# A fused attention, gated MLP and soft mixture of experts: the last two experts in column halves, and all output in half rows

## The chip, the cores and the metric

The kernel runs on one core of a Trainium2 chip, as one launch. Its engines are named as in the profile: PE (TensorE, matmul) and PEld (its weight loads), DVE (VectorE), ACT (ScalarE), POOL (GpSimd) and SP (SyncE, which issues the transfers here). The metric is the time of the launch in microseconds (us), lower is better. Several executions of the kernel are timed, and one more is profiled. All arithmetic is in fp32.

## What is computed

The reference has three stages, the output of each being the input of the next:

```python
# 1 attention: q, k, v of (4, 12, 448, 64), q and k normalised by their RMS
x = softmax(q_n @ k_n.T / 8) @ v               # laid out as (1792, 768)
# 2 gated MLP, d_ff = 1536
x = (silu(x @ w_gate) * (x @ w_val)) @ w_out   # (1792, 768)
# 3 soft mixture of experts: 8 experts, 4 slots each, F = 1024
logits = x @ phi                               # (1792, 32)
d = softmax(logits, over the tokens)
slot_input = (d.T @ x).reshape(8, 4, 768)
for e in range(8):
    h = maximum(slot_input[e] @ w1[e], 0)      # w1[e]: 768 x 1024
    slot_out[e] = h @ w2[e]                    # w2[e]: 1024 x 768
c = softmax(logits, over the slots)
out = c @ slot_out.reshape(32, 768)            # (1792, 768)
```

Only 32 rows go through the experts, but each expert has 6.3 MB of weights of its own, 50.3 MB for the eight.

## The kernel before

The first 660 us or so are attention and the MLP, which the change does not touch. What it touches is the tail, written between `eunits` (L975) and the end of the kernel.

**Units.** The expert weights are cut into 32 units of 1.5 MB, listed in `eunits` as (expert e, kind i, half n). Kind 0 is half of w1[e], by rows. Kind 1 is half of w2[e], by rows: 512 rows of all 768 columns. Kind 2 is a column half of w2[e]: all 1024 rows of 384 columns. A unit's place in the list is the order both of its load and of its computation. Experts 0 to 6 have kinds 0, 0, 1, 1; the last, expert 7, has kinds 0, 0, 2, 2.

**Loads.** `load_unit(u)` (L1000) issues unit u on the SP queue into one of 16 buffers (`unit_tile`, L984). The units take the buffers in turn; three of the 16 are made of two or four smaller tiles, and a unit that falls on one of those is loaded in as many pieces. A unit of kind 2 is loaded in four pieces of 384 KB, one for two of the eight row groups `kh`, with runs of 384 numbers (1,536 bytes) (L1028 to L1030). The first sixteen units are loaded ahead of the loop; unit u + 16 is issued after the computation of unit u, so the last loads are issued, in program order, after unit 15. The output buffers `ot[b]` and the combine weights `ct` take buffers of earlier units.

**The loop over units (L1647).** Kind 0: the 32 slot rows times w1[e], 24 matmul records for each half, into `hacc[e]`; after the second half ACT applies the relu (L1666), PE transposes (L1669), and DVE copies the expert's four slots into `h1m`, whose other columns are zero (L1673). Kind 1: `h1m` times w2[e] (L1684), accumulated over the experts in one PSUM tile `so`; after the last of them DVE copies `so` to `sall` (L1692). Kind 2: `slot_open(n)` puts the column half n of `sall` into a new PSUM tile `sl[n]` (an identity product, L1595); `slot_last(n, kh)` adds expert 7's products (L1602), for eight `kh` of four products each; `slot_out(n)` copies the sums to `sos[n]` in SBUF (DVE, L1612).

**Output.** `output(n, b)` (L1616) makes column half n of batch b: eight products of `ct` with `sos[n]` into four PSUM tiles (L1629), four copies to `ot[b]`, two on DVE and two on ACT (L1636), and transfers. Batch b's 448 rows lie on 112 partitions with four rows each. For batches 0 and 1 each column half goes out by itself, in two transfers of 336 KB with runs of 1,536 bytes (L1641). Batches 2 and 3 go out once, after their second half, as whole rows in one transfer of 1,344 KB (L1643). In total there are eight of the small and two of the large. `outs` sets the order: for n = 0 batches 0, 1, 2, 3, for n = 1 batches 2, 3, 0, 1. Three outputs of n = 0 are made between the products of the last unit:

```python
slot_open(n)
for kh_ in range(KH):
    slot_last(n, kh_)
    if n == 1 and kh_ in (1, 3, 5):
        output(*outs[0].pop(0))
```

the other five after the loop.

**Order.** The section is under a manual schedule: each engine's queue runs in program order, and the waits on semaphores follow from which tiles are read and written. Transfers are all issued by SP, on one queue, with eight semaphores taken in turn. `fill(k)` (L128) issues k groups of four bf16 products on a zero tile, which nobody reads; here it stands behind the units from number 22 on that are not of kind 2, with three groups, and one behind unit `NE - 3`.

Of the kernel before, what the change touches and what calls it, by code (L numbers as in the profile page):

```python
# [21 lines left out]
def attn_moe_softmoe_kernel(  # L22
# [15 lines left out]
    nc = tc.nc  # L38
    B, H, S, HD = q.shape
# [3 lines left out]
    E, _, F = w1.shape  # L43
# [7 lines left out]
    KH = F // P  # L51
# [920 lines left out]
    KD2, KH2 = KD // 2, KH // 2  # L972


    eunits = [(e, i, n) for e in range(E) for i in (0, 2 if e == E - 1 else 1) for n in range(2)]  # L975
    NE = len(eunits)

    NR, NL = (9, 2), 5
# [462 lines left out]
    TF = [22, 3, 3]  # L1441
# [108 lines left out]
    with tc.manual_schedule():  # L1550
        tp_ = tc.alloc_tile_pool(name="tail", bufs=1, side="left", reuse_waits="tile")
        pools.append(tp_)
        for u in range(NRT - NG, NRT - NG + NL):
            load_unit(u)
        rs = tp_.tile([P, 1], F32, name="rs")
        nc.vector.tensor_scalar(out=rs, in0=ssum, scalar1=EPS_SUM, scalar2=None, op0=ALU.add)
        nc.vector.reciprocal(out=rs, in_=rs)
        si = tp_.tile([P, DM], F32, tag="si", name="si")
        for n in range(2):
            o = si[:, DH * n : DH * n + DH].rearrange("q (c p) -> q p c", c=KD2)  # L1560
            src = sip[n][:, :DH].rearrange("q (p c) -> q p c", c=KD2)
            if n:
                nc.vector.tensor_scalar(out=o, in0=src, scalar1=rs[:, 0:1], scalar2=None, op0=ALU.mult)
            else:
                nc.scalar.activation(out=o, in_=src, func=AF.Copy, scale=rs[:, 0:1])
        for u in range(NRT - NG + NL, NRT + NL):
            load_unit(u)
        sit_ps = pt_tile("sit")
        for c in range(KD):
            nc.tensor.matmul(  # L1570
                sit_ps[:, NS * c : NS * c + NS],
                si[:, P * c : P * c + P],
                stack[:, 0, :],
                start=True,
                stop=True,
            )
        sit = tp_.tile([P, KD, NS], F32, name="sit")
        nc.vector.tensor_copy(out=sit, in_=sit_ps[:, : KD * NS].rearrange("p (c s) -> p c s", c=KD))

        warm_tag[0] = "s2"  # L1580
        DQ = DM // 4
        sos = [tp_.tile([P, DQ], F32, name=f"sos{n}") for n in range(2)]
        sall = tp_.tile([P, DQ], F32, name="sall")
        so = ps.tile([P, DQ], F32, tag="g", name="so")
        FQ = F // 4
        hacc, h1s = {}, {}
        ot = {}
        sl = []

        def slot_open(n):  # L1590

            sl.append(ps.tile([P, DQ], F32, tag="vg"[n], name="sl"))
            for j in range(4):
                m = 2 * n + j % 2
                nc.tensor.matmul(  # L1595
                    sl[n][NS * j : NS * j + NS, :], ident[:, NS * m : NS * m + NS], sall, start=True, stop=False
                )

        def slot_last(n, kh):

            for j in range(4):
                nc.tensor.matmul(  # L1602
                    sl[n][NS * j : NS * j + NS, :],
                    h1s[E - 1][:, kh, :],
                    w(kh, DQ * (j % 2), DQ),
                    start=False,
                    stop=(kh == KH - 1),
                )

        def slot_out(n):  # L1610

            nc.vector.tensor_copy(out=sos[n], in_=sl[n])  # L1612

        ops_n = [0]

        def output(n, b):  # L1616

            if b not in ot:
                ot[b] = unit_tile(NE + 1 + b).rearrange("p (c d) -> p c d", d=DM)[:CP]
            ops = []  # L1620
            for _ in range(4):
                k = ops_n[0] % 6
                ops_n[0] += 1
                ops.append(s_tile(k) if k < 3 else pt_tile("op"))
            for c in range(2):
                for j in range(4):
                    r = slice(NS * j, NS * j + NS)
                    o = S * b + CP * (c + j // 2 * 2)
                    nc.tensor.matmul(  # L1629
                        ops[j][:CP, DQ * c : DQ * c + DQ], ct_()[r, o : o + CP], sos[n][r], start=True, stop=True  # L1630
                    )
            ob = out[S * b : S * b + S].rearrange("(p c) d -> p c d", c=NC)
            cs = slice(DH * n, DH * n + DH)
            for j in range(4):
                h = slice(j // 2 * 2, j // 2 * 2 + 2)
                (nc.scalar.copy if j % 2 else nc.vector.tensor_copy)(  # L1636
                    out=ot[b][:, h, DH * n + DQ * (j % 2) : DH * n + DQ * (j % 2) + DQ],
                    in_=ops[j][:CP, : 2 * DQ].rearrange("p (c d) -> p c d", d=DQ),
                )
                if j % 2 and b < 2:  # L1640
                    nc.sync.dma_start(out=ob[:, h, cs], in_=ot[b][:, h, cs])  # L1641
            if b >= 2 and n:
                nc.sync.dma_start(out=ob, in_=ot[b])  # L1643

        outs = [[(n, (b + 2 * n) % B) for b in range(B)] for n in range(2)]

        for u, (e, i, n) in enumerate(eunits):  # L1647
            w = wtile.pop(u)
            if i == 0:
                if n == 0:  # L1650
                    hacc[e] = s_tile(e % 3)[:, :FQ]
                for c in range(KD2 * n, KD2 * n + KD2):
                    for j in range(4):
                        nc.tensor.matmul(  # L1654
                            hacc[e][NS * j : NS * j + NS, :],
                            sit[:, c, :],
                            w(c % KD2, FQ * j, FQ),
                            start=(c == 0),
                            stop=(c == KD - 1),
                        )  # L1660
                if n == 1:

                    h1m = tp_.tile([P, KH, NS], F32, tag="h1m", name="h1m", bufs=2)
                    nc.gpsimd.memset(h1m, 0.0)
                    hr = tp_.tile([P, FQ], F32, tag="hr", name="hr", bufs=2)
                    nc.scalar.activation(out=hr, in_=hacc.pop(e), func=AF.Relu)  # L1666
                    ht_ = pt_tile("htp")
                    for t in range(2):
                        nc.tensor.transpose(  # L1669
                            ht_[:, P * t : P * t + P], hr.rearrange("q (p t) -> q t p", t=2)[:, t], ident  # L1670
                        )
                    for t in range(2):
                        nc.vector.tensor_copy(  # L1673
                            out=h1m.rearrange("p (j t) s -> p t j s", t=2)[:, t, :, SPE * e : SPE * e + SPE],
                            in_=ht_[:, P * t : P * t + P].rearrange("p (j s) -> p j s", j=4)[
                                :, :, SPE * e : SPE * e + SPE
                            ],
                        )
                    h1s[e] = h1m
            else:  # L1680
                if i == 1:
                    for kh_ in range(KH2 * n, KH2 * n + KH2):
                        for j in range(4):
                            nc.tensor.matmul(  # L1684
                                so[NS * j : NS * j + NS, :],
                                h1s[e][:, kh_, :],
                                w(kh_ % KH2, DQ * j, DQ),
                                start=(e == 0 and kh_ == 0),
                                stop=(e == E - 2 and kh_ == KH - 1),
                            )  # L1690
                    if e == E - 2 and n == 1:
                        nc.vector.tensor_copy(out=sall, in_=so)  # L1692
                else:
                    slot_open(n)
                    for kh_ in range(KH):
                        slot_last(n, kh_)
                        if n == 1 and kh_ in (1, 3, 5):
                            output(*outs[0].pop(0))
            load_unit(u + NRT + NL)
            if u == 1:  # L1700
                combine1(tp_)
            if CB + 2 <= u < CB + 2 + B:
                combine3(u - CB - 2)
            if CB <= u < CB + B:
                combine2(u - CB)
            if i == 2:
                slot_out(n)
            elif TF[0] <= u:
                fill(TF[1 + i] // (2 if u == NE - 3 else 1))
        for a in outs[0] + outs[1]:  # L1710
            output(*a)
    tp_.release()
# [32 lines left out]
```

## Time and profile before

| what | value |
|---|---|
| time, median of 3 runs | 778.86 us (777.36 to 779.46) |
| the profiled execution's own time | 779.32 us |
| its span | 777.5 us |
| PE, DVE, ACT, POOL busy | 731.6, 464.8, 391.3, 437.2 us |
| mean granted clock of TensorE | 0.977 |
| read from and written to HBM | 136.84 MB, 19.66 MB |

The span is what the trace covers; the own time is that of the same execution as the launch sees it, 1.8 us more. Times in rows count from the span's start. A matmul row merges neighbours: "x16" are sixteen records, and an fp32 product leaves two of them. "SPq" rows are SP's issue instructions, which end when the transfer is handed over and not when the data have landed. "Idle before" in square brackets is the time that the engine stood idle ahead of the row, with what ended it. The DMA share is the mean busy share of the core's 16 DMA engines; it can come out slightly over 1.

### The profile page before, as it was taken

The numbers are of one execution on the slowest core, as the hardware profiler recorded it, in microseconds if no ns is written. First come the engines' busy times: TensorE is split into PE (matmuls) and PEld (weight loads), VectorE is DVE, ScalarE is ACT, GpSimd is POOL, SyncE is SP. The second block draws the span as 40 slices with busy tenths as digits, with TensorE's granted clock in tenths as the row PEclk, the third lists the DMA queues.
The fourth block names the chain that finished last, engine by engine and source line by source line (L and its number), as shares of the span: only waits on it lengthen the run. The fifth ranks groups of instructions, "written<-read, shape, count | busy, mean of one in ns | idle before, by whom it ended". The sixth has DMA issues, their size and how long they took to land.

```text
span 777.5 us, 20479 instructions
## 1 busy us (share of the span) xinstructions
PE 731.6 (94%) x8488; PEld 567.2 (73%) x8488; DVE 464.8 (60%) x918; ACT 391.3 (50%) x834; POOL 437.2 (56%) x379
## 2 busy tenths in 40 slices
PE   7799999999999999999999999999999999888782
PEld 5565657787777777888888788888878887555451
DVE  5989877788877876676677766666342223210012
ACT  5889878887797644454454445443222221201012
POOL 5987765767676866778685686746234442001000
PEclk8899999999999999999999999999999999999986
DMA  7677675755585642545334443235158788999977
GB/s 229 171 240 197 204 220 188 224 180 187 178 269 174 195 120 77 155 141 153 85 119 120 142 137 78 82 108 161 51 194 298 273 327 314 362 416 417 417 276 241
DMA packets 72221, 157.84 MB, mean 203 GB/s; under 512 B 9184, under 2 KB 45280, under 8 KB 70368
## 3 DMA queue, kind: packets, MB, share of 16 engines
q1 hardware_dynamic: 72128, 156.52, 60.5%
q8 instruction: 67, 1.10, 0.6%
q14 instruction: 26, 0.21, 0.1%
HBM read 136.84 MB, written 19.66 MB: 201 GB/s over the span
## 4 chain that ended last, share of the span: by engine, by line
PE 79%; DMA 7%; DVE 5%; issue 3%; POOL 3%; ACT 2%; DVEq 0%; SPq 0%; ACTq 0%; POOLq 0%
PE pg L711 43%; PE s L508 6%; PE xp L645 6%; DMA w<-in_moe_w_dram 5%; PE tp L587 3%; PE tq L439 2%; PE s L610 2%; PE xp L610 2%; PE s L1654 2%; PE lp L763 2%; PE s L512 2%; PE sp L840 1%; DMA qk<-in_k_dram 1%; PE wpp L267 1%; PE so L1684 1%
## 5 line engine op out<-in xcount | busy, mean ns | idle before, releaser
L711 PE MATMUL pg<-xh,wh 128*128 128x448 f32 x576 | 219.5, 381 | 0.0
L711 PE MATMUL pg<-xl,wh 128*128 128x448 f32 x576 | 209.9, 364 | 0.0
L535 ACT ACTIVATE pr<-s,sm 128x448 f32<-128x448 f32 x168 | 106.2, 635 | 110.8 <-DVE sm L523 108.4
L711 PE MATMUL pg<-xh,wl 128*128 128x448 f32 x432 | 157.9, 366 | 0.3 <-POOL wl L254 0.3
L711 PEld LDWEIGHTS pg<-xh,wh 128*128 128x128 f32 x576 | 108.2, 188 | 23.0 <-issue 12.2
L254 POOL TENSOR_TENSOR wl<-raw,wh 128x768 fp32r<-128x768 f32 x60 | 111.0, 1860 | 16.2 <-ACT wh L246 16.0
L711 PEld LDWEIGHTS pg<-xl,wh 128*128 128x128 f32 x576 | 108.5, 188 | 8.2 <-issue 0.6
L246 ACT CAST wh<-raw 128x768 fp32r<-128x768 f32 x96 | 78.9, 835 | 65.6 <-PE pg L711 34.3
L552 POOL TENSOR_SCALAR pr<-pr,su 128x448 f32<-128x448 f32 x84 | 54.5, 659 | 80.7 <-DVE su L548 34.7
L523 DVE TENSOR_REDUCE sm<-s 128x1 f32<-128x448 f32 x168 | 97.7, 613 | 2.7 <-PE s L508 0.9
L218 POOL TENSOR_TENSOR hpos<-hpos,hneg 128x768 f32<-128x768 f32 x36 | 66.1, 1836 | 37.1 <-ACT hneg L209 32.8
L711 PEld LDWEIGHTS pg<-xh,wl 128*128 128x128 f32 x432 | 81.2, 188 | 7.6 <-POOL wl L254 0.7
L732 DVE SCALAR_TENSOR_TENSOR ht<-ht,pg 128x448 f32<-128x448 f32 x48 | 29.7, 619 | 77.6 <-ACT ht L725 77.4
L254 POOL TENSOR_TENSOR raw<-raw,wh 128x768 fp32r<-128x768 f32 x24 | 44.1, 1840 | 51.2 <-ACT wh L246 51.2
L391 POOL TENSOR_TENSOR ri<-ss,mhalf 128x16 f32<-128x16 f32 (+2 forms) x24 | 67.3, 2802 | 2.0
L508 PE MATMUL s<-ka,qa 64*128 64x448 f32 x432 | 64.0, 400 | 1.7 <-DVE ka L65 0.9
L587 PE MATMUL tp<-ident,pr 128*112 128x128 f32 x336 | 51.6, 286 | 6.6 <-ACT pr L535 4.8
L631 DVE STREAM_TRANSPOSE pT<-pr 128x448 f32<-128x448 f32 x84 | 52.7, 628 | 5.3 <-POOL pr L552 5.1
L587 PEld LDWEIGHTS tp<-ident,pr 128*112 128x112 f32 x336 | 37.7, 137 | 23.4 <-ACT pr L535 8.6
L711 PE MATMUL pg<-xh,raw 128*128 128x448 f32 x144 | 52.7, 366 | 0.8 <-POOL raw L254 0.8
L508 PEld LDWEIGHTS s<-ka,qa 64*128 64x128 f32 x432 | 35.3, 186 | 23.1 <-issue 12.4
L413 POOL TENSOR_TENSOR qn<-qk,ri 128x512 f32<-128x512 f32 (+1 forms) x46 | 50.2, 1090 | 0.7
(190 smaller groups left out, 1158.4 us busy)
## 6 DMA issues: line engine op xcount, KB each, us to landing
w<-in_moe_w_dram SPq DMA_DIRECT2D x24, 1536.0 KB, 12.6
raw<-w SPq DMA_DIRECT2D x72, 384.0 KB, 4.9
w<-raw SPq DMA_DIRECT2D x36, 384.0 KB, 4.0
vt<-in_v_dram SPq DMA_DIRECT2D x60, 224.0 KB, 4.2
r<-in_moe_w_out_dram SPq DMA_DIRECT2D x12, 768.0 KB, 5.0
r<-in_moe_w_gate_dram SPq DMA_DIRECT2D x12, 768.0 KB, 5.3
r<-in_moe_w_val_dram SPq DMA_DIRECT2D x12, 768.0 KB, 5.9
w<-in_moe_w_dram SPq DMA_DIRECT2D x8, 768.0 KB, 15.1
```

The source lines that it names most:

```text
L218: eng.tensor_tensor(out=hp, in0=hp, in1=hn, op=ALU.subtract)
L246: (EV[ENG["wh1"]] if u - NO < NU else nc.scalar.copy)(out=wh, in_=wst[u]["raw"])
L254: eng.tensor_tensor(out=wl, in0=wst[u]["raw"], in1=wst[u]["wh"].bitcast(F32), op=ALU.subtract)
L391: nc.gpsimd.tensor_tensor(out=ri, in0=ss, in1=mhalf[:p, : len(ns)], op=ALU.pow)
L413: eng.tensor_tensor(out=st[i]["qn"][:, n].rearrange("p c h d -> p h c d"), in0=st[i]["qk"][: rows(i), n], in1=st[i]["ri"][:, n] .rearrange ...
L508: nc.tensor.matmul(sc[j], qa[r, wt, c * P : (c + 1) * P], ka[r, mv, :], start=(n == 0), stop=(n == 2))
L523: nc.vector.tensor_reduce(out=d["sm"][:, j : j + 1], in_=d["sc"][j], axis=AX.X, op=ALU.max, negate=True)
L535: nc.scalar.activation(out=p, in_=d["sc"][j], func=AF.Exp, bias=d["sm"][:, j : j + 1], accum_out=st[i]["su"][:, c, j : j + 1])
L552: nc.gpsimd.tensor_scalar(out=p, in0=p, scalar1=su[:, j : j + 1], scalar2=1.0, op0=ALU.mult, op1=ALU.mult)
L587: nc.tensor.transpose(tp[:CP, ck * P : (ck + 1) * P], pr[:, ck * CP : (ck + 1) * CP], ident)
L631: nc.vector.transpose(out=pT[:, 6 - c if j else c, :], in_=st[i][c]["pr"].pop(j))
L711: nc.tensor.matmul(d[r], wt[:, P * c : P * c + P], mv, start=(c == 0 and n == 0), stop=(c == KD - 1 and n == 2),)
```

## The change

The last two experts are treated alike. The list of units becomes: experts 0 to 5 as before; then both halves of the first weights of expert 6, then those of expert 7; then the first column halves of the second weights of experts 6 and 7, then the second column halves of the two. `so` and `sall` now end with expert 5. `slot_open(n)` runs at expert 6's column half, `slot_last` takes the expert as an argument, and `slot_out(n)` comes after expert 7's column half. During the second column halves of experts 6 and 7 an output of n = 0 is made ahead of `kh` 0 and `kh` 4, four in all, each ahead of two pairs of weight pieces. All batches now go out as half rows, sixteen transfers of 336 KB, in the order of the batches for both halves. The filling products end with unit 27 (`NE - 5`), which has one group.

```diff
@@ -972,7 +972,9 @@
     KD2, KH2 = KD // 2, KH // 2
 
 
-    eunits = [(e, i, n) for e in range(E) for i in (0, 2 if e == E - 1 else 1) for n in range(2)]
+    eunits = [(e, i, n) for e in range(E - 2) for i in range(2) for n in range(2)]
+    eunits += [(e, 0, n) for e in (E - 2, E - 1) for n in range(2)]
+    eunits += [(e, 2, n) for n in range(2) for e in (E - 2, E - 1)]
     NE = len(eunits)
 
     NR, NL = (9, 2), 5
@@ -1596,15 +1598,15 @@
                     sl[n][NS * j : NS * j + NS, :], ident[:, NS * m : NS * m + NS], sall, start=True, stop=False
                 )
 
-        def slot_last(n, kh):
+        def slot_last(e, n, kh, w):
 
             for j in range(4):
                 nc.tensor.matmul(
                     sl[n][NS * j : NS * j + NS, :],
-                    h1s[E - 1][:, kh, :],
+                    h1s[e][:, kh, :],
                     w(kh, DQ * (j % 2), DQ),
                     start=False,
-                    stop=(kh == KH - 1),
+                    stop=(e == E - 1 and kh == KH - 1),
                 )
 
         def slot_out(n):
@@ -1637,12 +1639,10 @@
                     out=ot[b][:, h, DH * n + DQ * (j % 2) : DH * n + DQ * (j % 2) + DQ],
                     in_=ops[j][:CP, : 2 * DQ].rearrange("p (c d) -> p c d", d=DQ),
                 )
-                if j % 2 and b < 2:
+                if j % 2:
                     nc.sync.dma_start(out=ob[:, h, cs], in_=ot[b][:, h, cs])
-            if b >= 2 and n:
-                nc.sync.dma_start(out=ob, in_=ot[b])
-
-        outs = [[(n, (b + 2 * n) % B) for b in range(B)] for n in range(2)]
+
+        outs = [[(n, b) for b in range(B)] for n in range(2)]
 
         for u, (e, i, n) in enumerate(eunits):
             w = wtile.pop(u)
@@ -1686,16 +1686,17 @@
                                 h1s[e][:, kh_, :],
                                 w(kh_ % KH2, DQ * j, DQ),
                                 start=(e == 0 and kh_ == 0),
-                                stop=(e == E - 2 and kh_ == KH - 1),
+                                stop=(e == E - 3 and kh_ == KH - 1),
                             )
-                    if e == E - 2 and n == 1:
+                    if e == E - 3 and n == 1:
                         nc.vector.tensor_copy(out=sall, in_=so)
                 else:
-                    slot_open(n)
+                    if e == E - 2:
+                        slot_open(n)
                     for kh_ in range(KH):
-                        slot_last(n, kh_)
-                        if n == 1 and kh_ in (1, 3, 5):
+                        if n == 1 and kh_ % 4 == 0:
                             output(*outs[0].pop(0))
+                        slot_last(e, n, kh_, w)
             load_unit(u + NRT + NL)
             if u == 1:
                 combine1(tp_)
@@ -1703,10 +1704,10 @@
                 combine3(u - CB - 2)
             if CB <= u < CB + B:
                 combine2(u - CB)
-            if i == 2:
+            if i == 2 and e == E - 1:
                 slot_out(n)
-            elif TF[0] <= u:
-                fill(TF[1 + i] // (2 if u == NE - 3 else 1))
+            elif i < 2 and TF[0] <= u:
+                fill(TF[1 + i] // (2 if u == NE - 5 else 1))
         for a in outs[0] + outs[1]:
             output(*a)
     tp_.release()
```

## Rows read from the trace of the kernel before

**Rows 1.** The page's head, and its DMA rate in 40 equal slices of the span (GB/s).

```profile
span 777.5 us, 20479 instructions
...
GB/s 229 171 240 197 204 220 188 224 180 187 178 269 174 195 120 77 155 141 153 85 119 120 142 137 78 82 108 161 51 194 298 273 327 314 362 416 417 417 276 241
```

**Rows 2.** TensorE and DMA by stretches: busy us of each engine, clock, DMA share, GB/s.

```profile
720.00:740.00 20.00, 14.26 (x223) 9.07 (x220) 0.61 (x3) 1.45 (x3) 0.31 (x1) 1.00 1.03 417
738.00:742.00 4.00, 1.62 (x29) 0.76 (x26) 0.00 (x0) 0.00 (x0) 0.00 (x0) 0.99 1.00 419
743.00:749.00 6.00, 4.65 (x42) 2.33 (x42) 0.26 (x2) 0.38 (x1) 0.00 (x0) 0.52 1.07 373
751.00:755.00 4.00, 4.00 (x92) 2.79 (x88) 1.38 (x3) 0.86 (x2) 0.00 (x0) 1.00 0.05 17
756.00:759.00 3.00, 2.99 (x60) 1.92 (x52) 2.04 (x5) 1.44 (x4) 0.00 (x0) 1.00 1.01 314
760.00:761.00 1.00, 0.79 (x18) 0.48 (x14) 0.98 (x2) 0.85 (x2) 0.00 (x0) 1.00 0.07 21
764.00:769.00 5.00, 0.00 (x0) 0.00 (x0) 0.75 (x2) 0.63 (x2) 0.00 (x0) 0.68 0.99 352
772.00:774.00 2.00, 0.00 (x0) 0.00 (x0) 0.00 (x0) 0.00 (x0) 0.00 (x0) 0.50 0.95 323
```

**Rows 3.** The chain of waits from 640 us: start us, us, what.

```profile
701.84 25.49 DMA w<-in_moe_w_dram
...
727.40 17.00 DMA w<-in_moe_w_dram
```

**Rows 4.** Timeline, SP queue from 725 us: start us, us, line, transfer, count.

```profile
729.27 15.68 SPq L1030 DMA_DIRECT2D w<-in_moe_w_dram  x8
754.41 2.71 SPq L1641 DMA_DIRECT2D out_dram<-w  x4
...
763.09 8.39 SPq L1641 DMA_DIRECT2D out_dram<-w  x4
```

**Rows 5.** Source lines 1030 (its issues, their landing) and 1641: ns min/median/max, starts.

```profile
L1030 SPq DMA_DIRECT2D w<-in_moe_w_dram x8: 540/546/5354, 729.3 to 744.4; - x8
...
DMA to landing us min/median/max: 8.2/13.6/16.2
...
L1641 SPq DMA_DIRECT2D out_dram<-w x8: 317/998/2632, 754.4 to 768.9; - x8
```

**Rows 6.** DMA issues of outputs at 754.41, 763.09, 768.9: KB, us to landing.

```profile
out_dram<-w SPq DMA_DIRECT2D x1, 336.0 KB, 2.8
...
out_dram<-w SPq DMA_DIRECT2D x1, 336.0 KB, 10.6
...
out_dram<-w SPq DMA_DIRECT2D x1, 336.0 KB, 7.7
```

**Rows 7.** Timeline, TensorE, four stretches of matmuls: start us, us, shape, count.

```profile
712.82 1.48 PE L1654 MATMUL s<-w,sit 128*32 128x256 f32 x24
...
744.44 2.79 PE L1654 MATMUL s<-w,sit 128*32 128x256 f32 x24 [0.79 <-DMA w<-in_moe_w_dram]
...
752.09 0.83 PE L1602 MATMUL sl<-w,h1m 128*32 128x192 f32 x16
...
753.70 0.86 PE L1602 MATMUL sl<-w,h1m 128*32 128x192 f32 x16
```

**Rows 8.** Timeline, VectorE, copies of the slot sums and of outputs.

```profile
752.01 0.36 DVE L1612 COPY sos<-sl 128x192 f32<-128x192 f32 x1 [3.15 <-PE sl L1602]
753.79 1.02 DVE L1636 COPY w<-s 112x384 f32<-112x384 f32 x2 [1.42 <-PE op L1629]
...
762.47 1.02 DVE L1636 COPY w<-s 112x384 f32<-112x384 f32 x2 [0.24 <-PE s L1629]
763.73 0.56 DVE L1636 COPY w<-op 112x384 f32<-112x384 f32 x1 [0.23 <-PE op L1629]
```

**Rows 9.** Waits of the SP queue from 725 us: us, times, longest.

```profile
SPq L1030 <- DMA w<-in_moe_w_dram: 7.5, 7, 3.1
```

## The prediction

> **What bounds the kernel now.** I read the page's head first, then the DMA rate by stretches, the chain of waits, the SP queue, and last TensorE and VectorE in the final 40 us. The slices of the page [rows 1] show a rate of 416 and 417 GB/s shortly before the end, falling to 276 and 241 in the last two. The stretches [rows 2] say what that is: from 720 to 740 us the queue moves 417 GB/s at a full share, from 743 to 749 us 373 GB/s, also at a full share, and then from 751 to 755 us only 17 GB/s. The chain [rows 3] names DMA alone for 701.84 to 744.40 us: the weights of the eight experts stream in, and everything else waits for them. So the weight stream sets the time until about 751 us. After it comes a hole, because the outputs cannot start: the reader is to see in the SP rows [rows 4] that the loads are issued by 744.95 us and the first output only at 754.41 us. In between TensorE does the last expert: its first-layer product at 744.44 us in 2.79 us, the relu and transposes, 64 slot matmuls, and the first combine products [rows 7]. From 754.41 us on the queue is fed piecewise: 21 GB/s from 760 to 761 us, since the two whole-row transfers wait for both column halves. The last four half-row transfers are issued from 763.09 us, the last one at 768.9 us, and it lands 7.7 us later, at 776.6 us [rows 4 to 6]; the span ends 0.9 us behind it.
>
> I therefore treat the tail as one queue: bytes at a known rate, plus holes.
>
> **Part 1: experts 6 and 7 by column halves.** No weight byte is added. The first weights of both experts come first (four units), then four units of column halves, two of which used to be whole-row units. Column-half pieces (384 KB, 1,536 B runs) go at 373 GB/s, the pieces before them at 417 [rows 2]. Two units are 3.146 MB: 8.43 us instead of 7.54, so 0.9 us more. The last weight landed at 744.4 + 8.2 = 752.6 us (the last start and the shortest landing [rows 5]) and now lands at 753.5. SP issues six more loads; its issue instructions run far ahead of the data (the last is done at 744.95 us, 7.7 us before that piece lands), so they are hidden. If that cover failed, each would cost its some 0.5 us.
>
> The pieces land 1.02 us apart (the first of the eight at 729.27 + 16.2 = 745.5 us, the longest landing; the last at 752.6 [rows 4, 5]), so the last piece of the first column half of expert 7 lands 8 x 1.02 us before the end, at 745.3 us, and expert 7's first layer arrives before all sixteen, at about 737.2. Between that product's end (747.23 us) and the first slot matmul's readiness (752.01 - 3.15 = 748.86) lay 1.6 us [rows 7, 8]; this now has some 5 us of room before expert 7's first half is due, and leaves the end's path. That is the heart of the change: before, 1.6 us of hand-over, 128 slot matmuls and the combine stood behind the last first-layer weight.
>
> **Part 2: TensorE behind the weights.** The slot matmuls are 256 instead of 128, but expert 6 no longer has its 64 + 64 in the old form, so the number of products is the same. Two chunks of 16 matmuls take 0.83 and 0.86 us, and from one chunk's start to the next there were 1.61 us with a batch's combine between them [rows 7], so that the combine takes 0.77 us (1.61 less a chunk's mean). From 745.3: a chunk 0.86, the copy of the slot sums 0.36 [rows 8], the combine 0.77, and 0.62 from the copy's start (753.79) to the issue (754.41) [rows 4, 8]. The first output transfer is issued at 748.0 us. Each further batch follows after two chunks and a combine, 2.46 us: 750.5, 752.9, 755.4. The last chunk ends at 746.6 + 4 x 2.46 = 756.4 us; it is TensorE's pace, not the landing at 753.5, that sets this. Copy, combine and eviction put the first transfer of the second half at 758.2, and the others follow at 1.26 us (762.47 to 763.73, VectorE's pace [rows 8]).
>
> **Part 3: all output as half rows.** Ten output transfers become sixteen of 336 KB. What one costs in a full queue: the last four landed from 763.09 + 10.6 = 773.7 to 776.6 us, 0.97 us each [rows 4 to 6]; 314 and 323 GB/s [rows 2] mean 1.10 and 1.07. I take 1.05. Whole rows went at 352 GB/s, so their 2.75 MB lose 0.7 us; this is within the 1.05.
>
> Are the outputs ever late? An output on an empty queue landed 2.8 us after its issue [rows 6]. If the queue runs on without a hole, output k lands at 753.5 + 1.05 k. Batch 0 needs its issue by 754.55 - 2.8 = 751.7 and has it at 748.0, 3.7 us early. The next have 3.3, 3.0 and 2.6 us, and the first of the second half 1.9 us (due at 760.1, there at 758.2). After that batches come every 1.26 us and leave every 2.1. SP's own waits: its column-half loads waited for the landing of earlier loads seven times [rows 9], one landing for each issue, eight apart; in that pattern output 1 waits for the piece that lands at 746.4 and output 8 for the last weight at 753.5, both before the data of those outputs are ready. All loads stand ahead of all outputs in SP's order, so no load waits behind an output's data. On an output that waits, only later outputs are queued.
>
> **Sum.** Last landing 753.5 + 16 x 1.05 = 770.3 us, 0.9 us to the end: a span of 771.2 instead of 777.5, 6.3 us less. Against its own time, 779.32, that is 773.0 us. The median of the runs is 778.86, inside their spread of 2.1 us; I leave the small difference to hand-overs that are not perfect. With 0.97 and 1.10 per transfer the sum gives 771.7 and 773.8.
>
> What the change costs on the queue is 0.9 + 0.7 us; what it fills is the hole from 751 to 755 us, the slow start and the second hole at 760.
>
> A rule that speaks against it: the Trainium skill (Perfetto Trace Analysis, DMA Optimizations) says that transfers under 2 KB carry a large overhead each and that batching them to 4 or 8 KB can raise throughput dramatically. By the rule the outputs should suffer most. The trace agrees in sign, with 373 against 417 GB/s for loads and 314 to 323 against 352 for stores [rows 2], but not in size.
>
> **Rivals.**
> *A, the clock dips once more (774.5 us).* From 738 to 742 us TensorE was busy 1.62 of 4.00 us, waiting for a 1.5 MB unit, and from 743 to 749 the granted clock was 0.52, half speed [rows 2]; 24 matmuls took 2.79 us there against 1.48 [rows 7]. The same idle stretch does not arise in the changed order (four small pieces instead of a large unit at that place, with 0.83 us of matmuls per 1.02 us), but the warm-up matmuls after these units are gone as well. A dip as long as the one seen, some 7 us, makes TensorE 3.4 us late; 1.9 us are free, so 1.5 us are left: 774.5.
> *B, half rows are dearer in a long row of them (776.5 to 781 us).* It eats the whole gain only if one takes 1.05 + 6.3/16 = 1.44 us, 239 GB/s; the slowest full stretch shows 314. Against it: four in a row kept 1.10.
> *C, slower: the clock stays at half from the first slot matmul on (785 us).* Chunks then take 1.69 us, more than the 1.02 us of a piece, and TensorE takes the place of the queue: 8 chunks from 739 us end at 752.5, then four times 4.9 us, copy, combine and eviction: the second half's first issue at 775.0, three batches at 1.5 us and a landing of 2.8 put the last landing near 782.8 and the time at about 785.5. It decides once TensorE loses over 6.3 + 1.9 = 8.2 us, which is more than 16 us at half speed. Against it: after the dense first-half products the clock is 1.00 from 751 us on [rows 2], and the new order is dense from 739.
> The Trainium skill (TensorE: Matmul & The Clock Gate, HAM oscillation) describes such a loop: compute shorter than the wait for its next slice throttles the array again and again. This trace shows the single dip.
> *D, outputs cut into the last loads.* The four transfers issued before 753.5 could delay the last weight by 4.2 us, to 757.7; the second half's first issue would then be 757.7 + 0.86 + 0.36 + 0.77 + 0.62 = 760.3, against a due time of 760.1: 773.2, no other result.
>
> **Chances.** The forecast with D, 771 to 774: 0.74. A and other small lateness, 774 to 776.5: 0.13. B or anything else that ends within 0.3% (2.3 us, about what this measurement can tell from no change): 0.07. C and slower: 0.06. So faster 0.87, same 0.07, slower 0.06. The range for 8 in 10 is 771.0 to 776.5: below it lies 0.97 us per transfer together with the median's 0.46 us, above it the dip with 1.10 us per transfer and a lost hand-over.
>
> **What the changed profile would show.** Right: no stretch below 280 GB/s between 740 and 768 us; slot matmuls from about 739 us and a clock of 1.00 through 757; first output issued near 748, last load landed near 753.5, last output near 770. Wrong: a hole around 752 or 760 (TensorE late, A or C: then the clock row says 0.5), output pieces over 1.2 us apart (B), or the last weight later than 755 (D).

## The result, and the profile after

The changed kernel took 768.96 us (median of 6 runs, 768.01 to 771.62), the kernel before in six runs 777.01 us (773.76 to 779.46): the ratio is 0.9903, with a 95% interval of 0.9873 to 0.9932. Timed once more, over 12 runs, it was 769.81 us against 774.77, a ratio of 0.9934 (0.9910 to 0.9959). The change is faster, as forecast, by 0.7 to 1.0%. The forecast of 773.0 us and its range of 771.0 to 776.5 are above the measured time.

The page's head and the DMA rate in 40 slices, of the changed kernel:

```profile
span 766.8 us, 20577 instructions
...
GB/s 232 167 244 188 224 224 194 229 176 189 163 271 195 195 99 104 146 132 141 84 123 156 145 81 81 116 132 132 84 145 241 316 305 335 310 415 417 416 376 308
```

The last two slices are 376 and 308 GB/s where they were 276 and 241 [rows 1]. The stretches tell the same in detail (columns as in [rows 2]):

```profile
700.00:726.00 26.00, 22.18 (x384) 14.42 (x378) 0.87 (x5) 2.90 (x6) 3.21 (x7) 1.00 1.02 419
736.00:742.00 6.00, 5.21 (x112) 3.02 (x108) 0.00 (x0) 0.00 (x0) 0.00 (x0) 1.00 1.07 373
745.00:749.00 4.00, 4.00 (x88) 2.63 (x84) 1.18 (x3) 0.97 (x3) 0.00 (x0) 1.00 1.08 382
750.00:754.00 4.00, 3.52 (x76) 2.47 (x68) 1.41 (x4) 0.86 (x2) 0.00 (x0) 1.00 1.05 374
755.00:764.00 9.00, 2.58 (x43) 1.65 (x36) 3.07 (x6) 2.58 (x6) 0.00 (x0) 0.77 0.98 314
```

Neither hole of [rows 2] is left: the DMA share is 0.98 or more in each of these stretches. Column-half loads go at 373 GB/s, as before. TensorE's clock is 1.00 as long as it has work in these stretches; there is no dip like that of 743 to 749 us in [rows 2]. New is the difference between the two output stretches, 374 GB/s and then 314. The first still holds the end of the loads; from 752 to 755 us, with outputs alone, the rate is 368.

The SP queue (start, duration, line, count), and the sources of its transfers with their issue times and time to landing:

```profile
721.87 20.33 SPq L1032 DMA_DIRECT2D w<-in_moe_w_dram  x16
744.58 17.68 SPq L1643 DMA_DIRECT2D out_dram<-w  x16
```

```profile
L1643 SPq DMA_DIRECT2D out_dram<-w x16: 317/422/1190, 744.6 to 761.7; - x16
...
DMA to landing us min/median/max: 4.1/5.2/8.1
```

The first output is handed over at 744.58 us, right behind the loads; before it was 754.41, 9.5 us behind them [rows 4]. The last load was issued at 741.65 us and landed 9.8 us later, at 751.4; six outputs stood in the queue by then. On TensorE and VectorE the chain that the prediction followed can be read directly:

```profile
738.59 1.84 PE L1604 MATMUL sl<-w,h1m 128*32 128x192 f32 x32 [0.27 <-DMA w<-in_moe_w_dram]
740.62 0.86 PE L1604 MATMUL sl<-w,h1m 128*32 128x192 f32 x16 [0.20 <-DMA w<-in_moe_w_dram]
...
751.04 1.51 PE L1604 MATMUL sl<-w,h1m 128*32 128x192 f32 x32
```

```profile
742.60 0.36 DVE L1614 COPY sos<-sl 128x192 f32<-128x192 f32 x1 [7.29 <-PE sl L1604]
743.95 1.02 DVE L1638 COPY w<-s 112x384 f32<-112x384 f32 x2 [0.99 <-PE op L1631]
...
752.62 0.36 DVE L1614 COPY sos<-sl 128x192 f32<-128x192 f32 x1 [0.47 <-PE sl L1604]
```

Up to 741 us TensorE waits for each piece (0.2 us at a time, ended by DMA); from the first copy of the sums on it waits for no load any more and sets its own pace to the second copy at 752.62.

**Two parts of the difference.** The profiled execution is 10.7 us shorter, more than the medians differ. A place up to which the two programs are the same is the last piece of expert 6's first weights; let M be its landing. The matmuls that wait for it, in the kernel before, in the changed kernel, and in the changed kernel's second profile:

```profile
729.26 1.06 PE L1654 MATMUL s<-w,sit 128*32 128x256 f32 x12 [0.82 <-DMA w<-in_moe_w_dram]
```

```profile
725.60 1.06 PE L1654 MATMUL s<-w,sit 128*32 128x256 f32 x12 [0.81 <-DMA w<-in_moe_w_dram]
```

```profile
729.05 1.06 PE L1654 MATMUL s<-w,sit 128*32 128x256 f32 x12 [0.77 <-DMA w<-in_moe_w_dram]
```

M is 729.2, 725.55 and 729.0 us. So 3.65 us of the 10.7 lie in M, up to which the two programs are the same, and 7.05 behind it: from M to the end of the span, which I call the tail, 48.3 us became 41.25. In the second profiles the tails were 47.6 (before) and 41.2 us (after).

### The profile page after: what moved, and what is told of

Same layout as the page of the kernel before. It is cut to its first block, busy times and chain, and to the rows that moved or that the text cites. A ratio compares the mean times of both kernels' runs of the same rounds, so it can differ in the third digit from the quotient of the medians.

```text
span 766.8 us, 20577 instructions
## 1 busy us (share of the span) xinstructions
PE 728.0 (95%) x8528; PEld 565.6 (74%) x8528; DVE 465.1 (61%) x918; ACT 391.7 (51%) x834; POOL 437.7 (57%) x379
## 4 chain that ended last, share of the span: by engine, by line
PE 77%; DMA 10%; DVE 4%; issue 3%; POOL 3%; ACT 2%; DVEq 0%; SPq 0%; POOLq 0%; ACTq 0%
PE pg L711 44%; DMA w<-in_moe_w_dram 8%; PE s L508 6%; PE xp L645 6%; PE tp L587 4%; PE tq L439 2%; PE xp L610 2%; PE s L610 2%; PE lp L763 2%; PE s L512 2%; PE sp L840 1%; PE wpp L267 1%; DMA qk<-in_k_dram 1%; PE rb L570 1%; DMA w<-raw 1%
## 5 line engine op out<-in xcount | busy, mean ns | idle before, releaser
L254 POOL TENSOR_TENSOR wl<-raw,wh 128x768 fp32r<-128x768 f32 x60 | 111.1, 1861 | 14.6 <-ACT wh L246 14.4
L587 PEld LDWEIGHTS tp<-ident,pr 128*112 128x112 f32 x336 | 37.0, 135 | 24.2 <-ACT pr L535 9.4
```

Of the source, the lines that this page charges most:

```text
L254: eng.tensor_tensor(out=wl, in0=wst[u]["raw"], in1=wst[u]["wh"].bitcast(F32), op=ALU.subtract)
L587: nc.tensor.transpose(tp[:CP, ck * P : (ck + 1) * P], pr[:, ck * CP : (ck + 1) * CP], ident)
```

## The experiments

Each is compared by its tail, which came out within 0.1 us in the two profiles of the changed kernel and within 0.7 in those of the kernel before, and by its ratio to the kernel before on the same chip. The tail of the first four expectations was counted from the copy of `sit`. That copy turned out a poor mark: it came at 674.7 to 681.0 us in the first six profiles without the weight stream moving along with it. The numbers below are from M; the differences that were expected carry over. Counted from the copy, as they were written, the four tails are 95.3, 95.3, 93.0 and 98.4 us.

| run | tail from M, us | first output issued, us after M | ratio to before (95%) |
|---|---|---|---|
| before, two profiles | 48.3, 47.6 | 25.2, 24.7 | 1 |
| changed, two profiles | 41.25, 41.2 | 19.0, 19.2 | 0.9903 (0.9873 to 0.9932), 0.9934 (0.9910 to 0.9959) |
| order_only | 45.0 | 19.0 | 0.9977 (0.9959 to 0.9995) |
| halves_only | 46.0 | 25.4 | 0.9969 (0.9947 to 0.9992) |
| late_out | 48.5 | 27.7 | 1.0014 (0.9996 to 1.0031) |
| two_queues | 40.9 | 19.0 | 0.9927 (0.9901 to 0.9952) |
| late_two | 50.8 | 28.3 | 1.0043 (1.0026 to 1.0060) |
| pe_late | 42.7 | 19.0 | 0.9952 (0.9932 to 0.9973) |
| one_expert | 45.2 | 24.2 | 0.9997 (0.9977 to 1.0017) |
| no_fill | 40.9 | 19.0 | 0.9942 (0.9921 to 0.9964) |
| one_per_half | 41.2 | 19.5 | 0.9935 (0.9914 to 0.9956) |

Each edited kernel has one profile, so its tail is one execution. In seven of the sets, the second one of the changed kernel among them, the ratio shows 0.8 to 2.9 us less gain than the tails do; no run shows where that difference lies.

**The kernel before again.** No edit.

> The kernel before, unchanged, profiled once more. Marker: the copy of `sit` on VectorE, with which the experts begin; head = span start to marker (678.4 us before, 674.7 after the change), tail = marker to span end (99.1 and 92.1). Theory H: the head is the same code in both kernels and only differs between executions (the kernel before had half-clock stretches at 114 and 670 us, the changed one had not); then head anywhere from 673 to 679, tail 99.1 +- 0.8. Rival: the change itself shortened the head by 3.7 us; then head 678.4 +- 0.5 again.

By the mark of this expectation theory H missed: the copy came at 678.9 us, in the rival's range, and the tail from it was 95.3 instead of 99.1. M decides it: it came at 726.5 us, 2.7 earlier than in the first profile of the same kernel, and the tail from it was 47.6. In all thirteen profiles of this text, of kernels with the same code up to M, M lies between 724.4 and 731.3 us. The rival falls: what lies ahead of M varies from execution to execution by 6.9 us, about as much as the change gains.

**The new order alone.**

```diff
-                if j % 2:
+                if j % 2 and b < 2:
                     nc.sync.dma_start(out=ob[:, h, cs], in_=ot[b][:, h, cs])
+            if b >= 2 and n:
+                nc.sync.dma_start(out=ob, in_=ot[b])
-        outs = [[(n, b) for b in range(B)] for n in range(2)]
+        outs = [[(n, (b + 2 * n) % B) for b in range(B)] for n in range(2)]
```

> The new order of experts and the interleaved outputs, but the old output form (batches 0, 1 as half rows, 2, 3 as whole rows at the end, old order of batches). Queue theory: after the last weight only four half-row transfers are ready, the queue runs dry for some 2.3 us until the whole rows come: tail 92.1 + 3.6 = 95.7 us (95 to 96.5), first output issued as in the changed kernel. Rival, the order alone makes the gain and the form of the output is of no weight: tail 92 to 92.8.

The tail is 3.75 us over the changed kernel's. The hole stands where it was expected, between the four half rows and the whole rows:

```profile
755.00:758.00 3.00, 3.00 (x68) 1.82 (x58) 1.33 (x3) 1.05 (x3) 0.00 (x0) 1.00 0.79 289
758.00:760.00 2.00, 1.23 (x20) 0.92 (x20) 0.94 (x3) 0.55 (x2) 0.00 (x0) 1.00 0.13 44
760.00:762.00 2.00, 1.76 (x31) 1.45 (x32) 1.53 (x4) 1.20 (x4) 0.00 (x0) 1.00 0.54 172
764.00:769.00 5.00, 0.00 (x0) 0.00 (x0) 0.21 (x1) 0.09 (x1) 0.00 (x0) 0.64 1.00 355
```

**Half rows alone.** The inverse edit, on the kernel before. It changes the form of the output and the order of the batches together; no run separates the two.

> The old order of experts with all output as half rows in the order of the batches. Queue theory: the hole behind the weights stays (first output 1.8 us after the last weight landed), but the second hole goes, and sixteen transfers of 0.97 to 1.10 us follow each other: tail 99.1 - 2.5 to 4.4 = 94.7 to 96.6 us. Rival, only the expert order matters: tail 99 +- 0.5.

A gain of 1.6 to 2.3 us in the tail, less than the 2.5 to 4.4 expected: the hole behind the weights stays, and the sixteen transfers land 1.12 us apart, not 0.97 to 1.10.

```profile
751.00:753.00 2.00, 2.00 (x44) 1.31 (x44) 1.25 (x3) 1.05 (x3) 0.00 (x0) 1.00 0.18 47
756.00:760.00 4.00, 3.26 (x56) 2.24 (x50) 3.25 (x7) 2.72 (x7) 0.00 (x0) 1.00 1.02 320
```

Each part alone brings some 3 and 2 us, both together 6.4 to 7.1.

**Outputs behind the last product.**

```diff
                     for kh_ in range(KH):
-                        if n == 1 and kh_ % 4 == 0:
-                            output(*outs[0].pop(0))
                         slot_last(e, n, kh_, w)
```

> The changed kernel, but all eight outputs are made after the last slot product instead of four between weight pieces. Queue theory: the queue runs dry when the weights end, the first output is issued some 2 us after the last weight has landed instead of 7 us before: tail 92.1 + 5.3 = 97.4 us (96.4 to 98.4). Rival, the bytes alone set the end: tail 92 to 92.8.

The whole gain is gone: a tail of 48.5 us, as in the kernel before. So the new order of the experts by itself gains nothing; it pays through the outputs that it lets issue while weights still load. The loss of 7.3 us is 2 us more than expected. The hole is there, and then the transfers land 1.14 us apart for the whole of the output:

```profile
753.00:756.00 3.00, 2.55 (x52) 1.50 (x44) 1.12 (x3) 0.72 (x2) 0.00 (x0) 1.00 0.00 0
757.00:774.00 17.00, 6.13 (x92) 4.28 (x92) 6.64 (x14) 5.55 (x14) 0.00 (x0) 0.76 1.00 303
```

**The changed kernel again.** No edit.

> The changed kernel, unchanged, timed beside the kernel before on one chip. New marker M: the first of the last twelve matmuls of expert 6's first layer (729.26 us before, 725.60 after), since the copy of `sit` came at 678 to 681 us in four further profiles while the weight stream behind it did not move; tail M = M to the span's end (48.2 before, 41.2 after). Theory H: the change works only behind M; tail M 41.2 +- 0.6, M itself anywhere between 725 and 732, and the median lies 6.4 to 7.1 us under the kernel before. Rival: it also shortens what lies ahead of M; then 8 us or more.

The tail repeats to 0.1 us, and M was 3.5 us later than in the first profile. The medians differ by 5.0 us here and by 8.1 in the first set; with the ratios' intervals both hold a gain of 6.4 to 7.0 us. The rival, something gained ahead of M, is not supported.

**Two queues.**

```diff
-                    nc.sync.dma_start(out=ob[:, h, cs], in_=ot[b][:, h, cs])
+                    (nc.scalar if n and j == 3 else nc.sync).dma_start(out=ob[:, h, cs], in_=ot[b][:, h, cs])
```

> The changed kernel, with every second output transfer of the second half issued from ScalarE's queue instead of SP's. In the changed kernel the transfers that SP issues one after the other take 0.85 to 1.2 us each to hand over there, and land 0.96 us apart, while the first half's, issued ahead, landed 0.87 apart. Theory I (the hand-over of one queue paces them): the second half lands 0.87 to 0.90 us apart, tail M 40.4 +- 0.3. Rival D (the write rate of the DMA engines paces them): 0.96 apart, tail M 41.2 +- 0.3. Rival: ScalarE's copies wait behind its issues, 41.5 and more.

The second half landed from 758.18 to 765.12 us, 0.99 apart: no gain. The tail of 40.9 us is inside the rival's range. The hand-over got shorter and the landing did not, so theory I is not what paces the output here.

**Two queues for late output.** The same with `j == 3` for both halves, on the kernel with late outputs.

> All eight outputs after the last slot product (as in the run with late outputs, tail M 48.5, sixteen landings 1.14 us apart), with every second transfer from ScalarE's queue. Theory I: landings about 0.9 apart, tail M 44.9. Rival D: 1.14 apart, tail M 48.5 +- 0.5.

1.24 us apart and a tail of 50.8, outside both ranges: slower still. Theory I falls. Of the 2.3 us over late_out, 0.6 lie ahead of the first output, which was issued 28.3 us after M instead of 27.7; that the second queue causes the rest is seen in this one profile.

**TensorE late.**

```diff
             if i == 2 and e == E - 1:
+                if n:
+                    fill(12)
                 slot_out(n)
```

> The changed kernel with 48 warm-up matmuls (some 3.3 us of TensorE) put ahead of the last copy of the slot sums. Prediction's margin: the second half's first transfer is issued 754.6 us and could land 2.8 us later, at 757.4, but lands at 759.1; so 1.7 us are free and the tail M is 41.2 + 1.6 = 42.8. Rival I (the hand-over paces the second half, so nothing is free): 41.2 + 3.3 = 44.5. Rival, the end is set by bytes alone: 41.2.

The fill took 2.85 us, partly beside the copy that TensorE waits for anyway, and put the second half's first issue 2.0 us later (31.1 us after M instead of 29.0). That transfer landed 0.3 to 0.6 us later, as a margin of 1.7 us allows. But the queue was short of work for a while, 243 GB/s at a DMA share of 0.68 from 752 to 756 us, and the seven behind it came 1.13 us apart instead of 0.96 to 0.99, so the tail grew by 1.5 us. The total agrees with the first expectation, the way there does not.

```profile
749.00:752.00 3.00, 3.00 (x64) 2.30 (x61) 1.38 (x3) 0.86 (x2) 0.00 (x0) 1.00 1.06 387
752.00:756.00 4.00, 3.68 (x68) 3.27 (x67) 1.02 (x2) 0.86 (x2) 0.00 (x0) 1.00 0.68 243
756.00:764.00 8.00, 2.47 (x40) 1.54 (x34) 3.06 (x6) 2.58 (x6) 0.00 (x0) 0.93 0.95 290
```

**Only expert 7 by column halves.**

```diff
-    eunits += [(e, 2, n) for n in range(2) for e in (E - 2, E - 1)]
+    eunits += [(E - 2, 1, n) for n in range(2)] + [(E - 1, 2, n) for n in range(2)]
-                        if n == 1 and kh_ % 4 == 0:
+                        if n == 1 and kh_ % 2 == 0:
```

(`so` and `sall` end with expert 6 again, `slot_open` is at expert 7.)

> A version meant to beat both: expert 7's first weights ahead of expert 6's second weights, but only expert 7 by column halves (expert 6's second weights as whole rows, at 417 instead of 373 GB/s), the four outputs of the first half each ahead of one pair of row groups of the last unit, output all as half rows. Queue theory with the measured prices: the weights end 0.9 us earlier; TensorE has only one unit to make four outputs in, so the first output of each half lands up to 0.4 us behind its turn: tail M 40.7 (40.3 to 41.2). Rival, one unit is too short a cover and TensorE paces the end: tail M 42 and more.

The rival holds, and more: a tail of 45.2 us. The weights landed at 24.8 us after M, no earlier than the 24.6 to 25.9 of the changed kernel. The first output came 5 us later and the queue ran dry. In the trace the products of expert 6's second weights start at 737.29 us, after a wait of 1.78 us that the landing of a 1.5 MB unit ended, and the clock dips as in the kernel before; that these two make the delay is read from the trace and not tested. The ratio of 0.9997 shows no gain in the time at all:

```profile
730.00:740.00 10.00, 6.71 (x78) 3.60 (x74) 0.26 (x2) 0.38 (x1) 0.00 (x0) 0.75 1.02 405
740.00:745.00 5.00, 5.00 (x92) 3.83 (x92) 0.36 (x1) 0.00 (x0) 0.00 (x0) 0.81 1.07 374
745.00:750.00 5.00, 4.85 (x108) 3.27 (x104) 1.39 (x4) 0.86 (x2) 0.00 (x0) 1.00 0.48 164
```

**No fill.** The calls of `fill` behind units 24 to 27 left out.

> The changed kernel without the warm-up matmuls behind units 24 to 27. Rival A of the prediction (a dip of the clock makes TensorE late, 1.7 us are free): a granted clock of 0.5 for some us between 728 and 745 and a tail M of 41.2 to 43. If the dense slot products alone hold the clock: no dip, tail M 41.2 +- 0.2.

No dip, and a tail of 40.9 us, 0.3 less. TensorE was idle for more than half of 728 to 732 us and the clock stayed:

```profile
728.00:732.00 4.00, 1.59 (x16) 0.70 (x14) 0.26 (x2) 0.38 (x1) 0.00 (x0) 1.00 0.98 404
736.00:740.00 4.00, 3.08 (x58) 1.93 (x59) 0.26 (x2) 0.38 (x1) 0.00 (x0) 1.00 1.07 372
```

**One transfer for each half.** `if j == 3:` and all four rows in the transfer.

> The changed kernel with one transfer of 672 KB for a batch's column half instead of two of 336 KB; the runs stay 1,536 bytes. If the bytes pace the output: landings 1.75 us apart and more, tail M 41.2 +- 0.4 (the first transfer of each batch starts some 0.5 us later, which the margin hides). Rival, a price for each transfer (0.1 us or more) is in the 0.90 us: tail M 40.4 or less.

The tail is 41.2 us again, and the landings are 1.92 us apart on average, twice 0.96. A price for each transfer is not in the 0.90 us; the bytes can be.

## Why the prediction was wrong

**The step that failed is the sum's base.** "Against its own time, 779.32, that is 773.0 us. The median of the runs is 778.86, inside their spread of 2.1 us": one execution, and three runs that lay close to it, were taken for the kernel's time. The next three runs of the kernel before took 773.76 to 776.67 us, and the medians on three further sets were 777.33, 774.77 and 775.57. The predicted 6.3 us less, off 777.01 us, are 770.7. The part of the execution ahead of M moves by some 7 us over the profiles, and the range gave it 0.46. Had it been given 3 us, the measured time would have been inside. Counted by M, the forecast is 729.2 + 42.0 and 1.8 us outside the span. The profiled execution of the changed kernel took 768.59 us, with M at 725.55 and a tail of 41.25: of the 4.4 us by which it came earlier, 3.65 lie in M and 0.75 in the tail.

**The gain itself was right in size and place.** 6.3 us was the sum; the tails shortened by 6.4 to 7.1, and the medians of the two sets of runs lie 8.05 and 5.0 apart. The terms, counted from M (729.2 in the prediction's frame):

| step | predicted | measured, two profiles |
|---|---|---|
| first output issued | 18.8 | 19.0, 19.2 |
| first output of the second half issued | 29.0 | 29.0, 29.0 |
| last weight landed | 24.3 | 25.9, 24.6 |
| sixteen outputs from there | 16.8 | 14.4, 15.6 |
| tail | 42.0 | 41.25, 41.2 |

That the tail came out so near is partly luck: in the first profile the last weight was 1.6 us later than forecast and the sixteen outputs 2.4 us shorter.

*TensorE behind the weights* was right to 0.4 us: the chunk, combine and copy durations of [rows 7, 8] carry over, and TensorE, not the last landing, ends the first half's outputs. *Expert 7's first layer off the end's path* was right: the last of its first weights landed at 733.2 us, `h1m` was ready at 735.3, and the first piece of its column half landed at 738.5. Calling it the heart of the change was too much: in late_out it is off the path as well, and nothing is gained without the early outputs.

*The price of an output*, 1.05 us, was too high: 0.90 and 0.97 on average. The prediction had 0.97 from four landings, and 1.10 and 1.07 from the 314 and 323 GB/s of [rows 2]. The 314 are from transfers issued as they were needed. The 323 are not: those four half rows were issued 7.7 to 10.6 us ahead, and they landed 0.87, 0.85, 1.18 and 0.86 us apart. In the changed kernel the first half's eight, which had waited behind the weights, landed 0.85 us apart, and in the other profiles with outputs ahead 0.82 to 0.85 on average, save for after_again (0.92) and one_per_half (0.96 for 336 KB), which have one long gap each. Those that follow a short queue take 0.96 to 1.01, and 1.1 to 1.14 where all were late. *The whole rows' advantage* of 0.7 us did not show in the first half: 1,536 B runs were written at 368 GB/s there, over the 352 of the whole rows in [rows 2]; the second half, at 314, stayed below it. The prediction weighed a rule on DMAs under 2 KB (the Trainium skill, Perfetto Trace Analysis, DMA Optimizations). The transfers here are of 336 KB and more, and only their runs are that short; as far as it may be read of runs, the loads agree in sign, 373 against 419 GB/s, and the first half's stores do not.

*The last weight* was 0.3 and 1.6 us later than the sum had it; in the first profile two of the sixteen column-half pieces landed 2.1 and 1.4 us behind the one before instead of 1.05, at a full DMA rate. No run was made to find out why, but the traces show a companion. Nine profiles have twelve such gaps of 1.3 us or more among these pieces, and each late landing came 2.2 to 2.8 us after the start of a 16 KB packet, some 1.1 us long, on the queue that the profile calls `instruction` (in the first profile at 742.35 and 748.88 us). Other such packets passed without a gap, so this is a correlation and not a cause that is shown.

**The rivals.** A did not come: the clock was 1.00 through the slot products, and no_fill shows that it does not hang on the filling. C did not come either, for the same reason. B fell: no transfer took over 1.2 us on average. D fell: in after_again the pieces kept landing 1.02 to 1.07 us apart after the first output had been issued, and late_out, which has no output ahead of the last weight, has an odd gap of 2.0 us too. In the first profile the larger gap (742.7 to 744.8 us) had nearly passed when the first output was issued at 744.58. The prediction counted four transfers issued before the last weight landed; six were. *The margins* were right for the start of the second half (1.9 us predicted, 1.7 measured), but lateness inside them was not free: pe_late lost 1.5 us in the transfers behind.

What stays open is why a transfer that has waited in the queue lands 0.85 us behind its predecessor and a late one 1.0 to 1.14. It is not the hand-over of one queue (two_queues, late_two) and not a price for each transfer (one_per_half). The wait itself is not shown as the cause either. The last four half rows of the kernel before and of order_only were issued 6.9 to 10.6 us ahead and landed 0.94 and 0.86 us apart on average, yet their bytes moved at 302 GB/s (770 to 774 us) and 311 (770 to 773 us). Landings and bytes part there: in the kernel before, the last two landed at 775.7 and 776.6 us, when from 775 us on only 16 GB/s moved.

## What to carry to other kernels

Where the end is a queue of transfers, look for the stretches in which the queue is dry, and order the last loads so that part of the output can be issued while loads still run; here filling two holes shortened the tail by 6.4 to 7.1 us, and neither part of the change filled both. A forecast of an absolute time needs the spread of the base, and one profile gives none: take the difference from the stage that changes, and the base, with its own width, from as many executions as there are.

## What the runs showed that was not expected

The first half's stores of 1,536 B runs, issued several us ahead, moved at 363 to 388 GB/s in four profiles, with no load beside them, about as fast as loads of the same run length (373):

```profile
754.00:758.00 4.00, 3.22 (x68) 2.15 (x60) 2.03 (x5) 1.47 (x4) 0.00 (x0) 1.00 1.06 388
759.00:768.00 9.00, 1.96 (x30) 1.33 (x28) 2.67 (x6) 2.23 (x6) 0.00 (x0) 0.82 0.97 306
```

These rows are of after_again, whose last load landed at 753.6 us. Stores issued as they were needed moved at 290 to 320 GB/s, at a DMA share of 0.95 to 1.02; so did the last four of the kernel before (302), which had waited. Issuing half of the late ones from ScalarE's queue did not help: 1.24 us apart in one profile, instead of 1.14.
